# A new tail for the table of order and engine in an attention and feed-forward kernel

## The chip, the cores and the metric

The kernel runs on one core of one Trainium2 chip. The metric is the device time of one execution in microseconds (us), the median of several runs. Five instruction streams matter: TensorE (PE; its weight loads are listed as PEld), VectorE (DVE), ScalarE (ACT), GpSimd (POOL) and SyncE (SP), which issues the transfers.

## The reference

`q`, `k` and `v` have the shape (4, 8, 768, 64): batch, heads, sequence, head size. Six sign bits of a projection put every query and key into a bucket, only pairs in one bucket attend, and the result goes through a feed-forward layer with Mish.

```python
mask = q_bucket[:, :, :, None] == k_bucket[:, :, None, :]
scores = scale * np.matmul(q, k.transpose(0, 1, 3, 2))
scores = np.where(mask, scores, -1000000000.0)
scores = scores - np.max(scores, axis=-1, keepdims=True)
attn = np.exp(scores)
attn = attn / (np.sum(attn, axis=-1, keepdims=True) + 1e-09)
attn_out = np.matmul(attn, v)
x = attn_out.transpose(0, 2, 1, 3).reshape(B * S, H * D)   # 3072 x 512
h = x @ w_in                                               # 512 -> 2048
g = h * np.tanh(softplus(h))
out = g @ w_out                                            # 2048 -> 512
```

## The kernel before

Numbers are split into a high and a low fp16 part, and a product is three fp16 matmuls (high by high, high by low, low by high). The tokens are worked in 12 units of 256 tokens. A unit has eight steps of attention and eight of the feed-forward layer, and the feed-forward steps of a unit run while the attention of the next one does. Unit 0 is done in fp32 while the weights are split.

The names below are those of the operations in the code.

- **S0 to S95** (`att_front`): the score products, 8 matmuls of line 894 each, into the one PSUM tile `ps_s` (three banks; some early ones use `ps_s2`). Then VectorE takes the maximum (line 906, `max`) and makes scale and bias (`scl`, lines 912 to 918), ScalarE takes two exponentials (line 932, `exp`), and only then may the next S overwrite the tile. `scl` is written as two VectorE instructions, as four shorter ones, or for GpSimd.
- After the exponentials come the reciprocal (954), a high part `hi` (line 387 on ScalarE, 388 on VectorE, 385 on GpSimd) and a low part `lo` (403) for each of the two heads, and a transposing transfer PT<-hl (420) on SP's queue.
- **V0 to V47** (`att_pv`): the value products, one for two S, 36 matmuls of line 1015 in 128 by 64 form, where nearly all others are 128 by 128. `x_hi` (1039, ScalarE) and `x_lo` (1042, VectorE) then empty their half of `ps_t`.
- **H0 to H95**, **O**: the first and second feed-forward products (lines 1075 to 1077; 1132 to 1134; in fp32 for unit 0, lines 1071 and 1128). Between them lie `mish` on ScalarE (1099), which needs another function table than the exponential, a high part (`g_hi`, 387 or 388) and a low part (`g_lo`, 403).
- Small things for the next batch or unit: sums of squares (437), their spread over the partitions by two small matmuls (`st`, 469 and 470, into `ps_t`), the step that reads them (`half`, 473), the hash products (`hp`, 728) with their bits (736) and the transfers KT<-tok and QT<-tok (420).

The order is written out. `op` records each of the 2978 operations with the engines that may do it and what must come before it. `ORDER` lists their numbers in the order in which they are issued, with a letter where it isn't the first engine that does it; `ordered` walks through it:

```python
for w in ORDER.split():
    n, a = (int(w[:-1]), "abcd".index(w[-1])) if w[-1].isalpha() else (int(w), 0)
    o = self.ops[n]
    yield o.alts[a][2]
```

Every engine takes its own operations in that order and waits for what it needs, so an operation that waits holds up all that stands behind it on its engine. Some entries are optional: `pre_e` and `pre_m` load a function table ahead of time, or do nothing in their second form, and `fill` is a set of 8 idle matmuls or nothing.

Of the kernel before, what the change touches and what calls it, by code (L numbers as in the profile page):

```python
# [99 lines left out]
404b 322 331 332 368b 413 511b 334 424b 335b 343 336c 337 414 512b 354b 355 362 363 357 369b 345 338 339 370b 356b 364  # L100
358 514b 359 420 223b 476 479 513 946b 366 371 367 344 386 394 374c 210b 478 532 372 387 375 360 361 373 389b 388b 395
425 505 506 396 390 481 376b 491 380b 515 381 377 398 391 392 399 426b 427 434 435 378 382 533 534 535 379 446b 428b
429 436b 531 393 488 530 438 430 439 536b 493 539b 468c 490 431 537c 432 433 440c 383 441 482 447 469 384 638 483 484b
385 470 448b 472 486 442 487 450b 473 594 494 597 540 443 516 497c 492b 471b 538 549 596 444 445 548 541 599 550 280b
551 474 451 452c 498 455b 449 406 453 500b 456 475 552 517 518b 604 499 1132b 457b 501 458 553b 556 554b 365b 545b
680b 520 407 454 558 607 521 559 555 503 557 495 405 585 542 522d 560 502 460 610 523 543 459 586 525 524b 461 587 544
526 588 464b 462b 973b 546 528 589 463 590c 465 466c 467 591 547 397b 609 527 504 584 569 561c 562 592b 624 756b 593
612 757b 408 758b 759b 570 409 563b 564b 571 641 529 565 572 626 642 627 760b 761b 625 762b 763b 764b 765b 766b 767b
768b 769b 770b 771b 772 773b 774b 628 775b 643 573 629 411 410 630 567 633c 631c 566 574 227b 665 676 575 576c 666 577
644 645 412 568 634 632 578 579 582 668 667 776 601 646 496 669 580 583 670 600 602 603 671b 674 672b 704 705 673 647b  # L110
648b 605 606 616c 613 581 693 675 650 706 713 684 694 649 685 635 651 617 618c 620b 695 686 683 737 636 687 637b 688b
# [12 lines left out]
1031 1032 959 903c 994 915 1096 906 1018 1019 1020 907 908 1083b 1631 1034 1035 938 1042b 1033 1051 1040 1052 1551b
909 1487b 1053 1626b 1011b 1240 1062 1064 995 1145 1036 1037 1055 996 997 998c 1000 1056 1070 1001 910 1131 1334b 1071
1072c 1133 1242 1141 931b 1136 1080 1074 1081 1082 1104 1138 1139c 1065c 1066 1140 1054 1134b 1073 1076 1085 1067 1148
1084 1097 1086 1087 1088c 1105 1106 1090 1115 786b 1068 1075 1256b 1089 1098 1099 999 1002 1003 1102 1004 1005 1153
1135 1169 1356b 1092 1101 1107b 1116 1108 1150 1077 1109c 1130 1170 1186 1091 1110c 1151b 1155 1185 1111 1119 1117
1118 1120 1121 1069 1006 1142 1156b 1113 1152 1208 1122 1123 1093 1124 1187 1112 1339b 1158 1154 1194 1125c 1128 1126
1195 1518 1143 1144 1157 1237 1146 1147 1171 1012 1161 1114 1159 1162 1163c 1160 1165 1129 1127 1209 1210 1164 1172  # L130
1173 1220 1176 1175 1177c 1211 1238b 1221 1379 1243 1167 1178 1179c 1027b 1188 1196 1181 1197 1198 1351b 1189 1190
1834 1248 1245 1259 1199b 1201 1246b 1247 1222 1250 1251c 1252 1380 1281 1297 1166 1180c 1183 1192 1193 1212 1213 1168
1214c 1216 1261 1444 1223 1224 1225 1228 1227 1202 1182 1215c 1218 1738b 1229b 1230 1262b 1263 1280 1296 1184 1231c
1233 1217 926 1264 1063b 1249b 1203 1137b 1232c 1266 1267b 1253 871b 1239 1254 1333 1255 1200c 1234 1204 1219 1338
1268 1335 1336b 1337 1235 1350 1257 1412 1206 1258 1272b 1282 1273 1340 1341b 1274 1244b 1283 1284 1286 1269 1236 1306
1275c 1276 1278 1287 1288b 1289 1290c 1292 1355 1299 1298 1305 1300 1149b 2311 1301 1307 1317 1205 1342 1352 1277 1291
1294 1100 1343 1332 1304 1303 1309b 1318 1279 1353b 1310 1270 1354 1381 1308 1319 1320 1311 1313 1293 1312 1315 1371
1382 1271 1322 1403 1372 1404 1323 1324b 1174b 1207 1295 1325 1326c 1328 1344 1357 1426 1314 1611b 1405 942 1316 1265b
1327 1345 1346 1360 1329 1358c 1349 1348 1383 1330 1331 1448 1376b 1359 1384 1385 2176b 1373 1361 1363 1364 1365 1386b
1387 1047b 1362 1374 1375 1377 1367 1378 1438 1439 1471 1427 1428 1388 1389 1406 1447 1395 1396 1799b 1429 1474 1397c  # L140
1399 816b 1366 1369 1058 1472 1407 1390 1391 1479 1476 1477b 1478 1413 1392 1414 1514 1408 1415 1368 1398c 1393 1480b
1481 1482c 1400 1513 1370 1416 1615 1490 1394 1417c 1419 1401 1420 1483 1411 1410 1430b 1441 1431 1433c 1546 1722 1402
1492 1432 1493c 1494 1473 1442 1443 1545 1547 1434 1435 1418 1285b 1191 1449 1421 1422 1423 1424 1445 1436 1446 1450
1463b 1605 1464 1465 1437 1425 1607 1451 1452 1608b 1453 1454b 1467 1468 1466c 1484 1495 1497 710 1485 1609 1486 1456
1521 1488 1498c 1469 1470 1499 1500 1503c 1489 1505c 1504 1506 1501 1734b 892b 1502 1625 1627 1515 1516 1610 1508 1511
1507 1509 1517 1555 1612 1457 1522 1613c 1558c 1572 1559 1614 1520 1519 1630 1537c 1538 1539c 1512 1548 1556 1557 1554
1510 1576 1541 1542 1549 1458 1459 1604 1455 1523 1540 1550 1543 1544 1524 1525 1526 1527 1528c 1460 1628b 1461 1553
# [1141 lines left out]
```

## Time and profile before

| | us |
|---|---|
| median of 3 runs | 822.91 (821.88 to 824.8) |
| the profiled execution, its own time | 822.01 |
| its span, first to last instruction | 820.2 |
| around the span | 1.8 |
| TensorE busy | 791.7 |
| VectorE busy | 700.9 |
| ScalarE busy | 661.7 |
| GpSimd busy | 64.0 |

Busy is the union of an engine's instructions. Matmuls overlap each other, so TensorE's busy time counts the time in which at least one is in flight. The granted clock of TensorE was 0.999 of the full 2.4 GHz over the span.

### The profile page before, as it was taken

To read this page: it belongs to the slowest core of one execution; us is meant where nothing else is said; L and a number is where in the kernel's file an instruction comes from. 1 tells how busy PE (TensorE), PEld (TensorE's weight loads), DVE (VectorE), ACT (ScalarE), POOL (GpSimd) and SP (SyncE) were. 2 spreads that over 40 slices of the span, in tenths; PEclk is the share of its full clock that TensorE was granted. 3 is DMA by queue.
4 is the path that set the end of the run, shared out by engine and by line. 5 is a ranking of instruction groups with operands and counts; after the bars stand their busy time and mean duration, and the time that the engine had idled before them with its cause. 6 is when DMAs were issued, how large, how long until landed. Compare 5 with 4: busy or idle time off the path is not lost. (4 is left out here: it accounts for less than half of the span.)

```text
span 820.2 us, 16787 instructions
## 1 busy us (share of the span) xinstructions
PE 791.7 (97%) x6588; PEld 547.3 (67%) x6588; DVE 700.9 (85%) x1349; ACT 661.7 (81%) x1000; POOL 64.0 (8%) x67
## 2 busy tenths in 40 slices
PE   6789999999999999999999999999999999999998
PEld 5566674666667676677677676676576577576664
DVE  6899999989889887889999888999899889789522
ACT  6899999989888789899797798788698788686312
POOL 3454441200000000000000000000000000000000
PEclk9999999999999999999999999999999999999999
DMA  9987979699999797999989779879979777866500
GB/s 266 274 248 223 230 180 188 141 164 215 177 178 172 144 185 129 157 190 189 214 155 200 152 131 178 167 130 215 181 143 196 141 109 125 142 118 128 109 1 26
DMA packets 400303, 135.58 MB, mean 165 GB/s; under 512 B 370528, under 2 KB 391008, under 8 KB 400224
## 3 DMA queue, kind: packets, MB, share of 16 engines
q1 hardware_dynamic: 400224, 134.52, 82.1%
q8 instruction: 51, 0.84, 0.4%
q14 instruction: 28, 0.23, 0.1%
HBM read 35.65 MB, written 6.29 MB: 51 GB/s over the span
## 5 line engine op out<-in xcount | busy, mean ns | idle before, releaser
L932 ACT ACTIVATE pb<-ps_s,svb 128x768 f32<-128x768 f32 x192 | 188.5, 986 | 38.2 <-DVE svb L918 31.4
L1075 PE MATMUL ps_acc<-X,wi 128*128 128x256 f16 x704 | 191.9, 273 | 1.0 <-ACT ffb L1099 1.0
L1077 PE MATMUL ps_acc<-X,wi 128*128 128x256 f16 x704 | 191.9, 273 | 0.0
L1076 PE MATMUL ps_acc<-X,wi 128*128 128x256 f16 x704 | 191.8, 273 | 0.0
L906 DVE TENSOR_REDUCE svb<-ps_s 128x2 f32<-128x1536 f32 x96 | 168.3, 1753 | 16.2 <-PE ps_s L894 14.8
L403 DVE SCALAR_TENSOR_TENSOR hl<-pb,svb,hl 128x768 f16<-128x768 f32 x175 | 176.2, 1014 | 6.5 <-ACT hl L387 4.4
L894 PE MATMUL ps_s<-KT,QT 128*128 128x512 f16 (+1 forms) x768 | 140.9, 326 | 7.5 <-ACT pb L932 2.8
L1132 PE MATMUL ps_o<-wo,ffb 128*128 128x512 f16 x352 | 133.5, 379 | 0.0
L1134 PE MATMUL ps_o<-wo,ffb 128*128 128x512 f16 x352 | 133.4, 379 | 0.0
L1133 PE MATMUL ps_o<-wo,ffb 128*128 128x512 f16 x352 | 133.4, 379 | 0.0
L894 PEld LDWEIGHTS <-QT 128*128 128x128 f16 x768 | 72.2, 97 | 56.1 <-issue 10.3
L1015 PE MATMUL ps_t<-PT,VT 128*64 128x256 f16 x1584 | 94.8, 274 | 2.2 <-DVE X L1042 1.5
L1099 ACT ACTIVATE ffb<-ps_acc,smalls 128x512 f32<-128x512 f32 x88 | 59.2, 684 | 43.9 <-PE ps_acc L1077 29.9
L1015 PEld LDWEIGHTS <-VT 128*64 128x64 f16 x1584 | 83.9, 110 | 16.1 <-issue 15.7
L387 ACT ACTIVATE hl<-pb,svb 128x768 f16<-128x768 f32 x78 | 71.7, 929 | 25.2 <-DMA PT<-hl 14.0
L1076 PEld LDWEIGHTS <-wi 128*128 128x128 f16 x704 | 68.8, 98 | 13.8 <-issue 1.6
L1075 PEld LDWEIGHTS <-wi 128*128 128x128 f16 x704 | 68.8, 98 | 12.1 <-issue 1.4
L1077 PEld LDWEIGHTS <-wi 128*128 128x128 f16 x704 | 68.8, 98 | 8.0
L403 DVE SCALAR_TENSOR_TENSOR ffb<-ffb,smalls 128x512 f16<-128x512 f32 x88 | 64.9, 746 | 3.3 <-ACT ffb L387 2.2
L1134 PEld LDWEIGHTS <-ffb 128*128 128x128 f16 x352 | 34.4, 98 | 41.5
L1133 PEld LDWEIGHTS <-ffb 128*128 128x128 f16 x352 | 34.4, 98 | 37.2
L1132 PEld LDWEIGHTS <-ffb 128*128 128x128 f16 x352 | 34.4, 98 | 34.2 <-issue 1.8
(208 smaller groups left out, 1038.2 us busy)
## 6 DMA issues: line engine op xcount, KB each, us to landing
out_dram<-ffb SPq DMA_DIRECT2D x24, 256.0 KB, 2.8
stg<-in_q_dram SPq DMA_DIRECT2D x10, 512.0 KB, 5.0
stg<-in_k_dram SPq DMA_DIRECT2D x12, 384.0 KB, 3.9
stg<-in_v_dram SPq DMA_DIRECT2D x12, 384.0 KB, 4.3
wo<-in_moe_w_out_dram SPq DMA_DIRECT2D x7, 512.0 KB, 4.3
stg<-in_moe_w_out_dram SPq DMA_DIRECT2D x7, 512.0 KB, 4.5
stg<-in_moe_w_in_dram SPq DMA_DIRECT2D x6, 512.0 KB, 5.3
wi<-in_moe_w_in_dram SPq DMA_DIRECT2D x6, 512.0 KB, 5.2
```

What stands on the lines that cost most here:

```text
L387: ACT=lambda: nc.scalar.activation(dst, src, AF.Copy, scale=sc),
L403: return [("DVE", 215 + 1.035 * n, port(lambda: nc.vector.scalar_tensor_tensor(out=dst, in0=src, scalar=sc, in1=hi, op0=ALU.mult, op1=ALU. ...
L894: nc.tensor.matmul(sc[:, hh * S + c0 * P:hh * S + c1 * P], QTb[:, u % 2, sl, qi], KTb[:, j, sl, hh * NCH + c0:hh * NCH + c1].rearrange("p ...
L906: op("max", [("DVE", 1790, lambda: nc.vector.tensor_reduce(out=sv[:, 0], in_=sc.rearrange("p (h e) -> p h e", h=2), axis=AX.X, op=ALU.max, ...
L932: EXP[n, hh] = op("exp", [("ACT", 1075, lambda hh=hh, t=t: nc.scalar.activation(pb[:, t], sc[:, hh * S:(hh + 1) * S], AF.Exp, bias=sv[:, 2 ...
L1015: nc.tensor.matmul(pv[hh * D:(hh + 1) * D, 0:256], vt[:, w, hh * NCH + c], pt[:, hh, a * NCH + c].rearrange("p s t -> p (s t)"), start=(x ...
L1075: nc.tensor.matmul(o, wh, X[:, 0, c], start=(c == 0), stop=False)
L1076: nc.tensor.matmul(o, wh, X[:, 1, c], start=False, stop=False)
L1077: nc.tensor.matmul(o, wl, X[:, 0, c], start=False, stop=(c == NCC - 1))
L1132: nc.tensor.matmul(PS[f"o{s}"], gh, hi[:, e], start=first, stop=False)
L1133: nc.tensor.matmul(PS[f"o{s}"], gh, lo[:, e], start=False, stop=False)
L1134: nc.tensor.matmul(PS[f"o{s}"], gl, hi[:, e], start=False, stop=last)
```

## The change

Only the string `ORDER` changes. Its first 361 entries are the same, which take about 66 us; from there to the end the entries are the same operations in another order and in part on other engines. No operation is added or removed, and TensorE does the same 556 groups of work (96 S, 48 V, 96 H, 192 O, 12 fills and the small ones). One line of 111 that differ:

```diff
-404b 322 331 332 368b 413 511b 334 424b 335b 343 336c 337 414 512b 354b 355 362 363 357 369b 345 338 339 370b 356b 364
+404b 223b 343 345 334 335b 413 322 331 545b 492b 280b 332 1132b 354c 336c 511 414 337 368b 355 573b 512b 638b 227b 356
...
```

Counted over the whole table, before and after: high parts of the attention weights 78, 87 and 11 on ScalarE, VectorE and GpSimd, now 76, 93 and 7; `scl` as two VectorE instructions 74, as four 20, now 66 and 28; high parts of the values 12 on ScalarE and 4 on VectorE, now 8 and 8; copies of the queries' high part 8 on ScalarE and 3 on VectorE, now 3 and 8; high parts of the feed-forward step 51 on ScalarE and 37 on VectorE, now 49 and 39; function tables loaded 108, now 117. The value products stand directly behind one another in 4 places, and now in 6.

Two places on VectorE show what moves. The first is ahead of S16, the first score product of unit 2, near 130 us. `L732` sums the hash product of that unit's queries, `L736` writes its bits into the token tile, which the transfer QT<-tok then turns; `L906`, `L912`, `L918` are the maximum and the scale step of S15, `L473` and `L458` the step behind a `st`. Before:

```order
L732 TENSOR_REDUCE hsum<-ps_t 128x96
L906 TENSOR_REDUCE svb<-ps_s 128x2
L403 SCALAR_TENSOR_TENSOR hl<-pb,svb,hl 128x768
L912 TENSOR_SCALAR svb<-svb,smalls 128x2
L918 TENSOR_TENSOR svb<-svb 128x2
L473 TENSOR_SCALAR hwo<-ps_t 128x2
L736 TENSOR_SCALAR tok_65<-hsum 128x16x6 x2
L458 TENSOR_SCALAR smalls<-hwo 128x2
L403 SCALAR_TENSOR_TENSOR hl<-pb,svb,hl 128x768
```

Now:

```order
L403 SCALAR_TENSOR_TENSOR hl<-pb,svb,hl 128x768
L732 TENSOR_REDUCE hsum<-ps_t 128x96
L906 TENSOR_REDUCE svb<-ps_s 128x2
L473 TENSOR_SCALAR hwo<-ps_t 128x2
L912 TENSOR_SCALAR svb<-svb,smalls 128x2
L918 TENSOR_TENSOR svb<-svb 128x2
L458 TENSOR_SCALAR smalls<-hwo 128x2
L736 TENSOR_SCALAR tok_65<-hsum 128x16x6 x2
```

The low part (`L403 hl`) between the maximum and the scale step is gone from there; it stands now ahead of the hash sum, so that the bits follow the hash sum and the maximum more closely. On TensorE, five O of unit 0 stand between S15 and S16 where there were four and two fills.

The second place is around S72 and V34, near 583 us. `L1042 X` is the `x_lo` that frees the half of `ps_t` that V34 writes; `L906` in the first list is the maximum of S72, and in the second the first `L906` is that of S71 and the last that of S72. Before:

```order
L388 TENSOR_SCALAR hl<-pb,svb 128x768
L403 SCALAR_TENSOR_TENSOR hl<-pb,svb,hl 128x768
L906 TENSOR_REDUCE svb<-ps_s 128x2
L912 TENSOR_SCALAR svb<-svb,smalls 128x2
L918 TENSOR_TENSOR svb<-svb 128x2
L782 TENSOR_REDUCE smalls<-smalls 128x1
L403 SCALAR_TENSOR_TENSOR hl<-pb,svb,hl 128x768
L473 TENSOR_SCALAR smalls<-ps_t 128x2
L1042 SCALAR_TENSOR_TENSOR X<-ps_t,smalls,X 128x256
L458 TENSOR_SCALAR smalls<-smalls 128x2
```

Now:

```order
L906 TENSOR_REDUCE svb<-ps_s 128x2
L912 TENSOR_SCALAR svb<-svb,smalls 128x1 x2
L916 TENSOR_SCALAR svb<-svb 128x1 x2
L736 TENSOR_SCALAR tok_65<-hsum 128x12x6
L403 SCALAR_TENSOR_TENSOR hl<-pb,svb,hl 128x768
L403 SCALAR_TENSOR_TENSOR ffb<-ffb,smalls 128x512
L1042 SCALAR_TENSOR_TENSOR X<-ps_t,smalls,X 128x256
L388 TENSOR_SCALAR hl<-pb,svb 128x768
L948 TENSOR_SCALAR svb<-svb 128x2
L403 SCALAR_TENSOR_TENSOR hl<-pb,svb,hl 128x768
L403 SCALAR_TENSOR_TENSOR ffb<-ffb,smalls 128x512
L906 TENSOR_REDUCE svb<-ps_s 128x2
```

`x_lo` stood behind the maximum of S72, a low part (`L403 hl`) and the `L473` of a `st`; it stands now ahead of the maximum of S72, behind the low part of an earlier step and a `g_lo`.

## Rows read from the trace of the kernel before

**Rows 1.** The page: busy time by engine; the chain that ended last.
```profile
PE 791.7 (97%) x6588; PEld 547.3 (67%) x6588; DVE 700.9 (85%) x1349; ACT 661.7 (81%) x1000; POOL 64.0 (8%) x67
...
PE 29%; DVE 1%; DMA 1%; ACT 0%; issue 0%; ACTq 0%
```

**Rows 2.** Windows: length, then busy us of each engine, clock, DMA share.
```profile
core 0: us, PE busy (x) PEld busy (x) DVE busy (x) ACT busy (x) POOL busy (x), PEclk, DMA share, GB/s
66.00:217.00 151.00, 143.79 (x1020) 96.79 (x1016) 144.47 (x256) 140.42 (x216) 32.99 (x26) 1.00 0.89 188
217.00:342.00 125.00, 124.33 (x1068) 85.95 (x1064) 108.87 (x214) 106.86 (x158) 0.00 (x0) 1.00 0.84 159
342.00:771.00 429.00, 426.18 (x3641) 293.71 (x3637) 381.97 (x723) 348.33 (x527) 0.00 (x0) 1.00 0.86 160
771.00:820.20 49.20, 45.24 (x330) 30.58 (x330) 12.10 (x20) 11.35 (x15) 0.00 (x0) 0.99 0.06 22
```

**Rows 3.** Waits of TensorE from 66 to 217 us: total, times, longest.
```profile
PE ps_s L894 <- ACT pb L932: 2.4, 4, 1.2
PE ps_s L894 <- DMA QT<-tok: 1.5, 1, 1.5
PE ps_acc L1075 <- ACT ffb L1099: 1.0, 2, 0.7
PE ps_t L469 <- ACT wo L437: 0.9, 1, 0.9
PE ps_t L1015 <- DMA PT<-hl: 0.4, 1, 0.4
PE ps_t L1022 <- ACT PT L978: 0.3, 1, 0.3
PE ps_t L1015 <- DVE hwo L473: 0.3, 1, 0.3
```

**Rows 4.** Waits of TensorE from 217 to 342 us, same columns.
```profile
PE ps_s L894 <- DVE smalls L458: 0.7, 1, 0.7
```

**Rows 5.** Waits of TensorE from 342 to 771 us, same columns.
```profile
PE ps_t L1015 <- DVE X L1042: 1.5, 1, 1.5
PE ps_t L728 <- DMA KT<-tok: 0.6, 1, 0.6
PE ps_s L894 <- ACT pb L932: 0.4, 1, 0.4
PE ps_t L469 <- ACT tok L437: 0.3, 1, 0.3
```

**Rows 6.** Timeline of VectorE: start, us, line, operation [idle before <-releaser].
```profile
583.39 0.15 DVE L782 TENSOR_REDUCE smalls<-smalls 128x1 f32<-128x4 f32 x1
584.65 1.02 DVE L403 SCALAR_TENSOR_TENSOR hl<-pb,svb,hl 128x768 f16<-128x768 f32 x1 [1.12 <-ACT hl L387]
585.59 0.15 DVE L473 TENSOR_SCALAR smalls<-ps_t 128x2 int32<-128x2 int32 x1
585.66 0.47 DVE L1042 SCALAR_TENSOR_TENSOR X<-ps_t,smalls,X 128x256 f16<-128x256 f32 x1
```

**Rows 7.** Timeline of TensorE: one value product alone, two in a row.
```profile
332.57 0.38 PE L1133 MATMUL ps_o<-wo,ffb 128*128 128x512 f16 x1
332.78 0.38 PE L1134 MATMUL ps_o<-wo,ffb 128*128 128x512 f16 x1
333.09 2.15 PE L1015 MATMUL ps_t<-PT,VT 128*64 128x256 f16 x36
335.18 0.18 PE L469 MATMUL ps_t<-smalls,ones 128*128 128x2 bf16 x1
...
437.84 0.38 PE L1134 MATMUL ps_o<-wo,ffb 128*128 128x512 f16 x1
438.15 4.12 PE L1015 MATMUL ps_t<-PT,VT 128*64 128x256 f16 x72
442.20 0.39 PE L894 MATMUL ps_s<-KT,QT 128*128 128x512 f16 x1
```

**Rows 8.** Timeline of TensorE around score product 16.
```profile
136.93 0.61 PE L1081 MATMUL ps_acc<-ones 128*128 128x128 bf16 x8
137.37 0.49 PE L894 MATMUL ps_s<-KT,QT 128*128 128x512 f16 x2
139.32 1.15 PE L894 MATMUL ps_s<-KT,QT 128*128 128x512 f16 x6 [1.45 <-DMA QT<-tok]
140.71 1.95 PE L1128 MATMUL ps_o<-wo,ffb 128*128 128x512 f32 x4
142.60 0.63 PE L1015 MATMUL ps_t<-PT,VT 128*64 128x256 f16 x8
```

**Rows 9.** Groups from 66 to 217 us: count, busy us, mean ns, idle before.
```profile
L388 DVE TENSOR_SCALAR hl<-pb,svb 128x768 f16<-128x768 f32 x5 | 3.1, 616 | 0.1
L912 DVE TENSOR_SCALAR svb<-svb,smalls 128x2 f32<-128x2 f32 x13 | 2.9, 224 | 0.3
L918 DVE TENSOR_TENSOR svb<-svb 128x2 f32<-128x2 f32 x13 | 2.1, 160 | 0.5
L912 DVE TENSOR_SCALAR svb<-svb,smalls 128x1 f32<-128x1 f32 x10 | 1.7, 209 | 0.1
L916 DVE TENSOR_SCALAR svb<-svb 128x1 f32<-128x1 f32 x10 | 1.7, 208 | 0.0
L388 DVE TENSOR_SCALAR ffb<-ffb,smalls 128x512 f16<-128x512 f32 x4 | 1.9, 474 | 0.0
L388 DVE TENSOR_SCALAR wi<-wi,smalls 128x1024 f16<-128x1024 f32 x3 | 2.2, 746 | 0.0
...
L385 POOL TENSOR_SCALAR hl<-pb,svb 128x768 f16<-128x768 f32 x11 | 15.7, 1431 | 33.3 <-DVE svb L954 18.3 <-DMA PT<-hl 8.2 <-ACT wi L437 6.7
```

**Rows 10.** Timeline of ScalarE around one table load.
```profile
408.38 0.19 ACT L932 ACTIVATION_READ_ACCUMULATOR pb<-ps_s,svb 128x1 f32 x1
408.59 1.28 ACT L1098 ACT_TABLE_LOAD   x1
409.88 0.69 ACT L1099 ACTIVATE ffb<-ps_acc,smalls 128x512 f32<-128x512 f32 x1
```

More of the change, by code (lines that the diff above doesn't have):

```diff
@@ new lines @@
+1153 1135 1169 1356b 1092 1101 1107b 1116 1108 1150 1077 1109c 1130 1170 1186 1091 1110c 1151b 1155 1185 1111 1119
+1117 1118 1120 1121 1069 1006 1142 1156b 1113 1152 1208 1122 1123 1093 1124 1187 1112 1339b 1158 1154 1194 1125c 1128
+1126 1195 1518 1143 1144 1157 1237 1146 1147 1171 1012 1161 1114 1159 1162 1163c 1160 1165 1129 1127 1209 1210 1164
+1172 1173 1220 1176 1175 1177c 1211 1238b 1221 1379 1243 1167 1178 1179c 1027b 1188 1196 1181 1197 1198 1351b 1189
+1190 1834 1248 1245 1259 1199b 1201 1246b 1247 1222 1250 1251c 1252 1380 1281 1297 1166 1180c 1183 1192 1193 1212 1213
@@ new lines @@
+1500 1394 1421 1605 1433c 1482c 1483 1435 1446 1484 1497 1503b 1513 1436 1437 1673 1463 1418c 1653b 1607 1496b 1422
+1464 1465c 1466c 1469 1470 1449 1450 1615 1467 1514 1493b 1423 1424 1468 1285 1451 1485 1452 1453 1454b 1486 1425
+1498c 1504 1456 1608c 1609 1546 1489 1488 1494 1625 1347b 1505c 1506 1507 1508 1515 1516 1517b 1555 1556 1519 1509
+1499 1940b 1520 1511 1557 1455c 1457 1522 1521 1610 1627 1510 1548 1545 1512 1547 1612 1458 1616 1537b 1538 1539c 1549
+1541 1523 1524 1501 1550b 710 1502 1558c 1459 1630 1540c 1543 1613c 1553 1552 1554 1525 1569 1568 1648 1560 1780b
@@ new lines @@
+1743b 1491b 1561 1632 1722b 1628b 1562 2231b 1542 1461 1526 1527 1460 1528c 1544 1462 1530 1570 1614 1531 1572 1563
+1564 1565 1629 1571 1566 1559 1575 1604 1635 1573 1576 1636 1633c 1574 1637 1596 1597 1598 1634 1599 1664 1600 1649
+1567 1619 1602 1601 1620 1621 1532 1665 1666 1701 1529 1577 1638c 1533 1578 1579 1687 1603 1591 1580 1623 1624 1650
+1581 1535 1582b 1688 1689 1534 1640b 1584 1651 1641 1642 1643 1690 1652 1654 1718 1644 1655 1585 1536 1726 1645 2059
+1586 1583 1480b 1674 1622b 1587 1646 1667 1721 1668 1656 1728 1719 1657 1658c 1669 1675 1676 1729c 1723 1660 1618
@@ new lines @@
+1860c 1863 1884 1939 1960 1941 1942c 2013 1931b 1932 1864 2061 1944 1943 1872 1873 1892 1893 1895c 1903 2014b 1886
+1894c 1896 2062 2063 1902 2015 1817b 1904 2089b 1898 1919 1899 1897 1905b 1885 1961 1887 2064 1946 1947b 2167 2018
+2016c 1949 1907 1908 1933 2017 1909b 1910 1911c 2023 1913 1934 1935 1912c 1948 1915 2030 1977 1976 1950 1937 1938
+1952b 1953 1954c 1956 2020 1962 1963 1978 1763 1997 2035 1964 1914 1955 1967 1966 1968c 1958 1969 1951 1916 1970c 1972
+1979 2032 1957 2037 1971 1965 1980 1981 1984 1983 1989c 2065 2021c 1985 2012 2038c 2033c 2022 2039 2066b 1986 1990
@@ new lines @@
+2310 2248 2284 2254 2299 2243c 2276 2246 2294 2300 2205 2206 2277 2207 2278c 2307 2280 2301 2328 2344 2329 2247 2281
+2345 2312 2308b 2309 2315 2019 2279 1982 2282 2283 2208c 2210 2209c 2304 2303 2155b 2316 2330 2346 2320 2321 2322
+2318c 2296 2211 1829b 2124b 2317 2255 2368 2331 2332 2239 2509b 2334 2324 2369 2367 2370 2335 2313c 2336b 2297 2337
+2338 2387b 2323 2256 2340 2326 2406 2347 2212 2353 2325 2314 2348 2213 2408 2257 2258 2409b 2401 2259 2422 2604b 2403
+2404b 2417 2327 2341 2339c 2349 2352 2351 2384 2342 2214 2260 2405 2261 2262c 2371c 2343 2264 2398 2265 2271 2373b
@@ new lines @@
+2460 2683 2682 2720 2721 2774b 2704 2731 2747 2749 2756 2684 2685 2686c 2687 2688 2690 2768 2703 2705 2706 2709 2708
+2733 2689 2723b 2724 2667 2423b 2691 2722 2668 2725 2727 2757 2734 2735 2551b 2950 2645 2758 2759 2955b 2738 2737
+2739c 2785 2786 2769b 2740 2726c 2728 2742c 2745 2746 2729 2730 2894 2788 2750 2793 2751 2752b 2741c 2790 2791b 2743
+2744 2932 2753b 2804 2889 2945b 2795 2796c 2797 2792 2754 2809 2755 2806 2771 2760 2761 2762c 2764 2811 2878 2826 2825
+2707 2772 2773b 2775 2763c 2807c 2766 2765 2776 2805 2777b 2798 2778 2779c 2781 2799 2800 2808 2880 2443 2767 2782
@@ L211 @@
+2879b 2919b 2920 2933 2925 2937 2770 2911b 2936 2938 2939 2514 2926 2949 2928 2171b 2934b 2929b 2930 2951 2944 2935
+2941 2943 2946 2952b 2953 2947c 2948 2959 2940 2942 2716b 2954 2915 2917 2031b 2912 2964 2966 2956 2694b 2961 2962c
+2963 2965 2967 2957c 2958 2968 2970 2971 2972b 2973 2969 2974 2976 2975b 2977
 """
```

187 lines of the change are left out of this document (77 added, 110 removed).

## The prediction, made before the changed kernel ran

> **What bounds the kernel now.** I read the page's busy times first [rows 1]. TensorE is busy 791.7 of 820.2 us, and the chain that ended last names it almost alone. So the question is not what any engine costs on average but where TensorE stands still, and whether the new order adds or removes such places. The windows [rows 2] cut the changed part into three and leave the tail. From 66 to 217 us TensorE is idle for 151 - 143.79 = 7.2 us, and VectorE has only 6.5 us to spare and ScalarE 10.6: three engines are nearly full, because the weights are split there. From 217 to 342 us TensorE is idle for 0.7 us, and from 342 to 771 us for 2.8 of 429. There VectorE has 47 us to spare and ScalarE 81. In the last 49 us TensorE runs at its own pace into the closing stores.
>
> All that a new order can win by waits is therefore 7.2 + 0.7 + 2.8 = 10.7 us, and two thirds of it lie in the stretch where VectorE is full. What it can lose has no such limit. The granted clock is 1.00 of 2.4 GHz in three windows and 0.99 in the tail [rows 2], so it plays no part.
>
> The lists of waits name nearly all of that idle time: eleven waits and 6.8 us in the first stretch [rows 3], one in the second [rows 4], four in the third [rows 5].
>
> **The change part by part.** TensorE's work is the same but for how often it changes form.
>
> *Changes to value products.* A value product alone costs two changes [rows 7]: the last O matmul starts 0.21 us after the one ahead of it, but V starts 0.31 after it, 0.10 more; and V then takes 335.18 - 333.09 = 2.09 us until the next product starts. Two V in a row take 442.20 - 438.15 = 4.05, where two alone would take 4.18. A pair thus saves 0.10 + 0.13, about 0.2 us. Two more pairs give **-0.4 us**. The bounds are narrow: 0.3 and 0.5.
>
> *342 to 771 us, waits that go.* All four listed waits [rows 5] sat at places where the order is now different. V34 waited 1.5 us for `x_lo` of V32. VectorE's rows show why it was late [rows 6]: `x_lo` (start 585.66) stood behind a low part that had waited 1.12 us for ScalarE's high part. The second pair of order lists has `x_lo` ahead of the maximum of S72, and so ahead of that low part and its wait: this one goes. The hash product that waited 0.6 us for KT<-tok stood directly behind H32; now H33, a `st` and H34 stand between, and one H is 24 matmuls at 0.11 us each, 2.6 us. S50 waited 0.4 us for its exponential with 4.6 us of other products since S49; now an O is added there. The `st` that waited 0.3 us for a sum of squares is moved too. I take all four as gone: **-2.8 us**. What is late next: in each of the four places, what follows on TensorE is ready. But some 400 us of new order make new waits, and these rows can't show where. The bounds are 0, and as many as the old order had times two, 5.6 us. I take a bit over half of the old, **+1.7 us**, since by my count the shortest distances are no worse: S to next S is 4.6 us of other work in 11 places before and in 11 now, and V stands at least 13.7 us of TensorE work behind its second S from V15 on, where the least was 13.0.
>
> *217 to 342 us.* From S31 to S42 the order is nearly the same, the 0.7 us wait [rows 4] included: **0**. VectorE has 16 us to spare there [rows 2]. It needs about 3.5 us more by S31, by the count of its instructions, and I cover that with this spare time; if it weren't there, the 3.5 us would be seen in full.
>
> *66 to 217 us, one wait that shrinks.* S16 stood still for 1.5 us in its middle for QT<-tok [rows 3, 8]. Now one more O of unit 0 and no fills stand ahead of it: an O takes up to 1.9 us with the change to V that follows it (140.71 to 142.60), two fills at most 0.4 us each (136.93 to 137.37), so S16 has about 1 us more to cover, or somewhat more. On VectorE the bits that the transfer needs stand closer behind the hash sum (first pair of lists), but the hash sum itself is later; by adding up VectorE's instructions from the start of the change, the bits come some 0.6 us later. I take the difference as **-0.7 us**, between 0 and -1.5.
>
> *66 to 217 us, more work on VectorE.* Until S26, which starts at 217.1 us, I counted what VectorE must have done in either order. It has six more high parts, about 0.62 us each (one of weights 0.75) [rows 9]: +3.8. Four scale steps are written as four short instructions (2 x 0.209 + 2 x 0.208 = 0.83) in place of two (0.224 + 0.160 = 0.38): +1.8. Three fewer high parts of the feed-forward step, 0.474 each: -1.4. The small ones give -0.2. That is +4.0 us in nine more instructions; instructions on VectorE begin about 0.08 us before the one ahead ends (584.65 + 1.02 against 585.59) [rows 6], which leaves **+3.2 us**. ScalarE's sum is the same within 0.2 us, and GpSimd does four high parts less, which took it 1.4 us each and for which it waited 33 us in all [rows 9]. So work goes from the one engine with time to spare to the fullest one. The cover is VectorE's 6.5 us of idle time. If it takes all of the new work, the cost is nothing, or a gain where a slow GpSimd step no longer holds up a transfer; if nothing fits, it is the whole 3.2. Four of the score products in this stretch waited for the exponentials that follow VectorE's scale step [rows 3], so the slack is thin. I take **+1.2 us**, a bit over a third, with ends at -2 and +3.2.
>
> *Function tables.* Nine more loads on ScalarE, 1.28 us each by the row [rows 10], 11.5 us. By the order, the additional ones fall behind 500 us, where ScalarE has most of its 81 us to spare [rows 2], or in the tail, where it is busy 11 of 49 us: **0**. If each stood in the chain from an S to the next, it would cost the full 1.28.
>
> The sum: -0.4 - 2.8 + 1.7 + 0 - 0.7 + 1.2 + 0 = **-1.0 us**. It applies to the profiled execution's 822.0 us (820.2 of span and 1.8 around it) and gives 821.0; against the median of the runs, 822.9, it gives 821.9. I put it in between, at **821.5 us**.
>
> About 0.3%, 2.5 us, is what a measurement of this kernel can tell from no change: faster means under 820.4, slower over 825.4.
>
> **The rivals.**
>
> *Faster: the order fits throughout.* The four later waits go and few new ones come (+0.5 in place of 1.7), and of the 7.2 us that TensorE idles from 66 to 217 us some 3 go, because high parts that waited on GpSimd are done at once elsewhere. That gives -0.4 - 2.3 - 3 = -5.7, about 817 us. For it speaks that VectorE's 6.5 us of idle time would hold all of the new work twice over; against it that VectorE is 96% busy there and gets more.
>
> *Slower: VectorE decides the first stretch.* If its idle time stays 6.5 us, because it is made of short waits at fixed places, S26 comes 3.2 us late and S31 3.5 us, and nothing gives it back, since TensorE is full from 217 us on. With -0.4 and new waits as long as the old ones (0): 822.9 + 3.1 is 826 us. It decides from the point at which less than about 1 of those 3.2 us finds room. Against it: ScalarE's part and the order of the low parts are eased at the same time.
>
> *Slower: the tables stand in the chain.* Near the end a load stands between an exponential and the high part behind it, though one did so before. If all nine were on TensorE's path, 822.9 + 11.5 = 834 us. Against it: only TensorE's 2.8 us of waits from 342 to 771 us name ScalarE at all, 0.7 us of them. The Trainium skill's ScalarE page (ScalarE: Activation LUTs, What ACT_TABLE_LOAD costs) gives a further drain of about 1.38 us to each load, 2.66 in all, by which nine would take 24 us of ScalarE. The trace doesn't agree: the load starts at 408.59, takes 1.28, and the next activation starts at 409.88 [rows 10].
>
> *No change that can be seen* is my forecast's own case: many small sums of both signs.
>
> **How the numbers follow.** The forecast, within 2.5 us of before: 0.43. Faster: 0.37, since four waits are seen to go and only guesses come in their place. VectorE as the bound: 0.16, and the tables: 0.04, together 0.20 for slower. The range reaches from the faster rival's 817, less 0.5 for a ramp that gains a little more, to the slower one's 826: 816.5 to 826.
>
> **What would show it.** TensorE's waits from 342 to 771 us should not name `X` L1042 with 1.5 us nor KT<-tok behind H32, and should sum to about 2. From 66 to 217 us (to the start of S26) TensorE's idle time should stay at 7 to 8 us; QT<-tok should wait under 1 us; VectorE should be busy for 147 to 148 us. V pairs should stand in six places at 4.05 us. If S26 starts after 220 us, the second rival is right; before 215, the first. A table load just ahead of an exponential for which an S waits would show the third. I would be wrong altogether if new waits of a kind that these rows don't show, such as transfers that land later because others are issued ahead of them, came to more than 3 us.

## The result, and the profile after

The changed kernel takes 829.8 us (median of 4 runs, 827.62 to 830.74), before on the same chip 822.62: a ratio of 1.0079 (95% interval 1.005 to 1.0108). It is slower by some 6.5 us, and outside the predicted range. The profiled execution takes 829.13 us with a span of 827.2, 7.0 more than before.

The page of the changed kernel: busy time by engine, and the chain that ended last.

```profile
PE 793.9 (96%) x6588; PEld 548.6 (66%) x6588; DVE 704.1 (85%) x1383; ACT 664.3 (80%) x1002; POOL 60.1 (7%) x62
...
PE 52%; DVE 12%; ACT 7%; DMA 5%; issue 2%; SPq 0%; ACTq 0%; DVEq 0%
```

Against [rows 1] no engine has much more to do. What has changed is the chain: it leaves TensorE more often. The shares of the two pages can't be compared as they stand, since the chain of before reaches back only to 562 us (its shares make 31%) and that of the changed kernel to 174 us (78%). From 568 us on, where both have one, TensorE holds 241 of 249 us before and 212 of 256 now, VectorE 6 and now 26, transfers none and now 11.

The windows of the changed kernel, cut at the same points of the program as [rows 2]:

```profile
66.00:219.70 153.70, 144.13 (x1030) 96.86 (x1028) 149.40 (x265) 141.33 (x218) 29.33 (x23) 1.00 0.89 188
219.70:343.60 123.90, 123.90 (x1056) 85.42 (x1052) 109.17 (x212) 103.80 (x157) 0.00 (x0) 1.00 0.81 158
343.60:777.80 434.20, 428.03 (x3642) 295.11 (x3638) 382.76 (x753) 348.42 (x523) 0.00 (x0) 1.00 0.86 157
777.80:827.20 49.40, 45.21 (x331) 30.54 (x330) 9.22 (x15) 15.90 (x21) 0.00 (x0) 1.00 0.06 22
```

The lengths differ from [rows 2] by +2.7, -1.1, +5.2 and +0.2 us, 7.0 together. In the first stretch TensorE now idles 153.7 - 144.13 = 9.6 us, where it was 7.2, and VectorE is left 4.3 us, where it was 6.5. In the third TensorE idles 6.2 us, where it was 2.8.

TensorE's waits in that third window, total, times and longest:

```profile
PE ps_t L728 <- DMA QT<-tok: 2.4, 1, 2.4
PE ps_s L894 <- ACT pb L932: 1.6, 4, 0.7
PE ps_t L1015 <- DMA PT<-hl: 1.2, 1, 1.2
PE ps_acc L1075 <- ACT ffb L1099: 0.8, 2, 0.5
```

None of the four waits of [rows 5] stands in its old place: that part of the prediction came true. But new ones take more than their room. The largest is a hash product that waits for QT<-tok. Here it is on TensorE's timeline (start, us, operation, idle before it), where the reader should look at what comes behind it too:

```profile
363.14 0.58 PE L728 MATMUL ps_t<-pj,QT 128*128 128x12 f16 x16 [2.40 <-DMA QT<-tok]
363.58 0.38 PE L1075 MATMUL ps_acc<-X,wi 128*128 128x256 f16 x1
363.75 0.42 PE L1076 MATMUL ps_acc<-X,wi 128*128 128x256 f16 x1
363.96 0.42 PE L1077 MATMUL ps_acc<-X,wi 128*128 128x256 f16 x1
...
366.69 0.27 PE L1075 MATMUL ps_acc<-X,wi 128*128 128x256 f16 x1
366.80 0.27 PE L1076 MATMUL ps_acc<-X,wi 128*128 128x256 f16 x1
```

H36's matmuls start 0.21 us apart instead of 0.11 until 366.5: TensorE stood still for 2.40 us, and then ran at half clock. The window from 363.0 to 366.6 says so, at 0.53 of 2.4 GHz:

```profile
363.00:366.60 3.60, 3.46 (x31) 2.59 (x32) 2.15 (x6) 1.39 (x2) 0.00 (x0) 0.53 1.10 235
```

H36's 24 matmuls take 1.47 us longer than at full clock. So this one place costs 2.40 + 1.47 = 3.9 us. It isn't the whole loss: the one run of the four whose mean granted clock was 1.000 took 827.62 us, still 5 us over before, and the others, at 0.996 to 0.998, took 829.1 to 830.7.

Why the transfer is late is seen on SP's queue. First before, then after (start, us on the queue):

```profile
350.84 1.45 SPq L420 DMA_TRANSPOSE KT<-tok  x1
353.59 1.79 SPq L420 DMA_TRANSPOSE QT<-tok  x1
355.47 2.02 SPq L420 DMA_TRANSPOSE PT<-hl  x1
```

```profile
351.42 5.29 SPq L420 DMA_TRANSPOSE PT<-hl  x2
356.82 1.72 SPq L420 DMA_TRANSPOSE QT<-tok  x1
358.64 2.30 SPq L420 DMA_TRANSPOSE KT<-tok  x1
```

KT<-tok is issued 7.8 us later than before, and QT<-tok 3.2 us later, both behind two PT<-hl that hold the queue for 5.29 us. Of either delay 1.6 us is the whole program's: S42 starts that much later. VectorE is caught as well. Its copy of the queries' high part, which the new table takes from ScalarE here, waits for KT<-tok with everything behind it:

```profile
364.38 0.43 DVE L397 COPY tok<-tok 128x1024 f16<-128x1024 f16 x1 [2.58 <-DMA KT<-tok]
```

And the transfers themselves take longer. From issue to landing, in the same 24 us of the program, before and after (count, median us):

```profile
PT<-hl SPq DMA_TRANSPOSE x6, 3.9
KT<-tok SPq DMA_TRANSPOSE x2, 4.4
QT<-tok SPq DMA_TRANSPOSE x2, 4.5
```

```profile
PT<-hl SPq DMA_TRANSPOSE x6, 4.7
KT<-tok SPq DMA_TRANSPOSE x2, 5.4
QT<-tok SPq DMA_TRANSPOSE x1, 6.3
```

The first stretch, waits of TensorE from 66 to 219.7 us; beside [rows 3] the wait for QT<-tok went from 1.5 to 0.4, and that of the score products for their exponentials from 2.4 to 4.6:

```profile
PE ps_s L894 <- ACT pb L932: 4.6, 5, 1.4
PE ps_t L469 <- ACT wi L437: 1.3, 2, 0.7
PE ps_t L1015 <- DMA PT<-hl: 1.1, 2, 0.9
PE ps_t L728 <- DVE X L1042: 0.9, 1, 0.9
PE ps_s L894 <- DMA QT<-tok: 0.4, 1, 0.4
```

### The profile page after: what moved, and what is told of

It is laid out like the page before. It is cut to its first block, busy times and chain, and to the rows that moved or that the text cites. A ratio compares the mean times of both kernels' runs of the same rounds, so it can differ in the third digit from the quotient of the medians.

```text
span 827.2 us, 16807 instructions
## 1 busy us (share of the span) xinstructions
PE 793.9 (96%) x6588; PEld 548.6 (66%) x6588; DVE 704.1 (85%) x1383; ACT 664.3 (80%) x1002; POOL 60.1 (7%) x62
## 4 chain that ended last, share of the span: by engine, by line
PE 52%; DVE 12%; ACT 7%; DMA 5%; issue 2%; SPq 0%; ACTq 0%; DVEq 0%
PE ps_s L894 8%; PE ps_t L1015 7%; PE ps_o L1132 7%; PE ps_o L1134 6%; PE ps_o L1133 6%; PE ps_acc L1075 6%; PE ps_acc L1076 6%; PE ps_acc L1077 6%; DVE svb L906 3%; DVE hl L403 3%; DMA PT<-hl 3%; ACT pb L932 3%; DVE hl L388 1%; ACT hl L387 1%; DVE ffb L403 1%
## 5 line engine op out<-in xcount | busy, mean ns | idle before, releaser
L403 DVE SCALAR_TENSOR_TENSOR hl<-pb,svb,hl 128x768 f16<-128x768 f32 x175 | 178.3, 1025 | 6.1 <-ACT hl L387 4.5
L906 DVE TENSOR_REDUCE svb<-ps_s 128x2 f32<-128x1536 f32 x96 | 168.1, 1751 | 9.5 <-PE ps_s L894 9.0
L403 DVE SCALAR_TENSOR_TENSOR ffb<-ffb,smalls 128x512 f16<-128x512 f32 x88 | 64.8, 745 | 21.4 <-ACT ffb L387 20.5
L387 ACT ACTIVATE hl<-pb,svb 128x768 f16<-128x768 f32 x76 | 69.6, 930 | 14.6 <-DMA PT<-hl 6.9
L1134 PEld LDWEIGHTS <-ffb 128*128 128x128 f16 x352 | 34.4, 98 | 42.2 <-DVE ffb L403 0.9
L388 DVE TENSOR_SCALAR hl<-pb,svb 128x768 f16<-128x768 f32 x93 | 57.7, 625 | 2.8 <-DMA PT<-hl 1.4
L1133 PEld LDWEIGHTS <-ffb 128*128 128x128 f16 x352 | 34.4, 98 | 36.7
```

Source lines behind the costliest of these rows:

```text
L387: ACT=lambda: nc.scalar.activation(dst, src, AF.Copy, scale=sc),
L403: return [("DVE", 215 + 1.035 * n, port(lambda: nc.vector.scalar_tensor_tensor(out=dst, in0=src, scalar=sc, in1=hi, op0=ALU.mult, op1=ALU. ...
L906: op("max", [("DVE", 1790, lambda: nc.vector.tensor_reduce(out=sv[:, 0], in_=sc.rearrange("p (h e) -> p h e", h=2), axis=AX.X, op=ALU.max, ...
L1133: nc.tensor.matmul(PS[f"o{s}"], gh, lo[:, e], start=False, stop=False)
L1134: nc.tensor.matmul(PS[f"o{s}"], gl, hi[:, e], start=False, stop=last)
```

## The experiments

Two theories stood at first. **Transfers:** the loss lies in single places, above all the middle piece, where transfers are issued late. **VectorE:** the loss is the work given to VectorE in the full first stretch. A third was open: that of the function tables. Ratios are to before on the same chip; 0.001 is 0.8 us.

| kernel | median us | ratio, 95% interval |
|---|---|---|
| e1_first | 824.39 | 1.0008, 0.9995 to 1.0022 |
| e2_middle | 827.11 | 1.0047, 1.003 to 1.0063 |
| e3_last | 823.75 | 1.0008, 0.9994 to 1.0022 |
| e4_queue | 829.4 | 1.0071, 1.0055 to 1.0087 |
| e5_hp_later | 827.54 | 1.0052, 1.0036 to 1.0068 |
| e6_engines | 839.93 | 1.0204, 1.0179 to 1.0229 |
| e7_orderonly | 848.76 | 1.0307, 1.0284 to 1.0329 |
| e8_mends | 822.25 | 0.9991, 0.9978 to 1.0004 |
| e9_copy_later | 828.56 | 1.0068, 1.005 to 1.0087 |
| e10_v35 | 828.32 | 1.0064, 1.0046 to 1.0082 |
| e11_before_mended | 823.45 | 1.001, 0.9996 to 1.0025 |
| e12_turns_early | 830.41 | 1.0094, 1.0075 to 1.0112 |
| e13_old_middle | 825.06 | 1.003, 1.0016 to 1.0044 |
| e14_turn_late | 830.43 | 1.0083, 1.0062 to 1.0104 |

**Which piece.** The table differs in three pieces, between which the same operations have been issued in both orders, so each can be taken alone.

```diff
-before
+before[:361] + after[361:1107] + before[1107:]     (e1_first)
+before[:1386] + after[1386:1793] + before[1793:]   (e2_middle)
+before[:1927] + after[1927:]                       (e3_last)
+after[:1386] + before[1386:1793] + after[1793:]    (e13_old_middle)
```

> The new order only up to S30 (entries 362 to 1107 of the table), the old one from there. In the two traces S31 to S40 start 2.4 us later than before. If VectorE's added work in the first stretch makes that, this is 2 to 3 us over before, and TensorE idles 9 to 10 us up to S26 in place of 7.2. If the loss is all from transfers that land late later on, or from the function tables, it is within 1 us of before.

> The new order only between S41 and S54 (entries 1387 to 1793). In the traces this stretch loses 3.9 us net: 2.4 us of a wait for QT<-tok, 1.5 us of matmuls at half the clock right behind that wait, some waits of 0.4 to 0.7 us, against 1.9 us of old waits that go. If a stretch's loss is its own, this is 3.5 to 4.5 us over before, with the same wait and the same dip of the clock. If the wait came from the state in which the first stretch left the queues, it is not here, and the time is 1 us or more under before.

> The new order only from S59 on (entries 1928 to the end); seven of the nine added table loads lie here. In the traces this stretch loses 0.5 us: V34's wait of 1.5 us goes, V35 waits 1.5 us for PT<-hl, and smaller ones come. If that is its own, this is within 1 us of before. If the tables cost, each up to 1.28 us, it is 2 us or more over before.

> The changed kernel with the order of before in the middle piece alone (S41 to S54, 342 to 446 us). Theory A (the middle piece holds the loss, 3.5 us by itself and 2 to 2.5 more where the new first piece stands ahead of it): 823.5 to 824.5 beside before's 823, as the first and last pieces alone, each about 0.5 us over. Theory B (what the first piece loses on VectorE shows in full when the middle piece is well): 825.5 to 827.

The middle piece alone costs 0.0047, 3.9 us; the first and the last 0.7 us each, neither distinct from nothing. With the old middle piece the changed kernel is at 1.003: of its 6.5 us over before some 4 are gone, and 2.5 are left. Against before, theory A gave 0.5 to 1.5 us over and theory B 2.5 to 4: the 2.5 stand at the lower edge of theory B, so more of the loss lies outside the middle piece than I had taken. The traces show where. S8 stands ahead of the change and S42 at the start of the middle piece; their rows on TensorE, first before, then after:

```profile
63.66 1.46 PE L894 MATMUL ps_s<-KT,QT 128*128 128x512 f16 x8
342.12 1.47 PE L894 MATMUL ps_s<-KT,QT 128*128 128x512 f16 x8
```

```profile
63.59 1.46 PE L894 MATMUL ps_s<-KT,QT 128*128 128x512 f16 x8
343.76 1.46 PE L894 MATMUL ps_s<-KT,QT 128*128 128x512 f16 x8
```

From S8 to S42 is 278.46 us before and 280.17 after. The same in three stretches and for the exchanged pieces, us more than in the trace of before:

| trace | S8 to S42 | S42 to S58 | S58 to the end |
|---|---|---|---|
| changed kernel | +1.7 | +4.6 | +0.7 |
| e1_first | +1.4 | -0.1 | +0.8 |
| e2_middle | -0.2 | +3.0 | +1.0 |
| e3_last | 0.0 | 0.0 | +1.4 |
| e13_old_middle | +1.6 | -0.2 | +1.0 |

The first piece therefore has a price of its own: in the eight traces with it (these and those of the kernels below) S8 to S42 takes 1.0 to 2.3 us more than in the trace of before, in the four others with the old one from 0.8 less to 0.1 more. With before itself that is 1.8 us apart in the mean. In the last column e1_first and e2_middle, with the old order there, are as long as the changed kernel, so it shows no clear loss of the last piece. Alone and in company the middle piece isn't quite the same: by itself its hash product waits 1.6 us for QT<-tok and the half clock doesn't come; behind the new first piece it waits 2.40 and 1.47 follow.

```profile
PE ps_t L728 <- DMA QT<-tok: 1.6, 1, 1.6
```

The last piece also holds the additional table loads: from 500 us on e3_last loads 54 tables, before 44 and the changed kernel 55 (the four groups of ACT_TABLE_LOAD added up). Its time is within 0.0022 of before.

**Places in the middle piece.** In the first edit QT<-tok (1420) goes ahead of a PT<-hl (1402) on SP; in the second the waiting hash product (1421) goes behind H36 (1605); in the third, on top of it, the copy (1418) and the hash sum (1422) go later on VectorE; in the fourth, on top of that, V35 (2368) and its `x_hi` (2369) go behind an O (2367).

```diff
-1402 1420 1500            (e4_queue)
+1420 1402 1500
...
-1421 1605 1433c           (e5_hp_later)
+1605 1421 1433c
...
-1418c 1653b 1607 1496b 1422 1464 1465c 1466c 1469 1470 1449      (e9_copy_later)
+1653b 1607 1496b 1464 1465c 1466c 1422 1469 1470 1418c 1449
...
-2368 2331                 (e10_v35)
...
-2369 2367 2370
+2367 2368 2369 2370
```

> The changed kernel with one entry moved: the transfer QT<-tok for unit 6 is issued ahead of a PT<-hl that stood before it on SP's queue. In the trace its data were ready at 354.7 us and it was issued at 356.8, behind a pair of PT<-hl that held SP for 5.3 us. If the queue makes the 2.4 us wait, the wait shrinks to under 0.5 us, the clock stays up behind it, and the time falls by 2.5 to 4 us against the changed kernel. If the transfer itself lands late because the DMA engines are full, the wait stays over 1.5 us, and the time within 1 us.

> The changed kernel with one entry moved: the hash product that waits 2.40 us for QT<-tok at 363.1 us is issued behind H36 instead of ahead of it. Theory A (its place on TensorE costs 2.47 us of standing still and, by the half clock behind that, 1.47 us more in H36): 3.9 us less than the changed kernel, 825.5 to 826, and H36's matmuls at 0.109 us a step. Theory B (the transfer queue is the limit, as when the two transfers were exchanged): the same wait turns up behind H36 or at the next value product, and the time stays above 828.5.

> The kernel with the hash product behind H36, and on VectorE the copy of the next queries' high part, which waits 2.26 us there for KT<-tok with everything behind it, moved behind the reciprocal, two high parts, the hash sum and a low part. Theory A (the copy is given to VectorE by the new table and holds up S44's maximum, so that S45 stands still for 1.76 us): that wait is gone, S46 starts 1.5 to 2 us earlier against its own start, and the time is some 1.7 us less, 825.8 beside 827.5. Theory B (S45 is late for another reason, say its exponential on ScalarE): S45 still waits over 1 us and the time stays within 0.6 us.

> The same, and V35, which waits 1.25 us for PT<-hl near 593 us (1.54 us with what else stops in it), moved behind the next feed-forward product. Theory A (its place ahead of the landing is all): the wait is gone and the time is some 1.4 us less than with the copy moved alone, about 824.4. Theory B (what follows V35 on the other engines, the low part of S74 and the hash product, is late next): S74 or the value products up to V37 wait by as much, and the time stays within 0.5 us.

With QT<-tok ahead, the hash product no longer waits, but V20 does, for the PT<-hl that was put behind, and half clock follows there too; the time is as long as before the exchange:

```profile
PE ps_t L1015 <- DMA PT<-hl: 2.5, 1, 2.5
```

With the hash product behind H36 the wait and the half clock are gone, and S44 starts about 4 us earlier against the score products ahead of it. Then S45 stands still, because VectorE still waits for KT<-tok and its maximum comes late, and with it the exponential (the row names a `g_hi` of VectorE that ended at the same moment). Of that kernel a row of the waits from 343 to 450 us, and one of VectorE's timeline:

```profile
PE ps_s L894 <- DVE ffb L388: 1.6, 1, 1.6
```

```profile
365.26 0.43 DVE L397 COPY tok<-tok 128x1024 f16<-128x1024 f16 x1 [2.26 <-DMA KT<-tok]
```

So 3.9 us were to be had and about 2 were won by the ratio, 1.0052 beside 1.0079; the intervals overlap, but the trace shows both halves. With the copy moved out of the way too, S45 waits 0.7 us, and a small product 1.9 us for a square on ScalarE, which in the code must come behind the copy, and so is late with it: VectorE now waits 2.90 us for PT<-hl ahead of the copy. No time was won (1.0068):

```profile
PE ps_t L469 <- ACT tok L437: 1.9, 1, 1.9
```

V35's move took its wait for PT<-hl away and nothing off the time (1.0064): a `st` near 604 us and H43 lose 0.6 us each in that trace, where they lost none in the one of the copy moved alone. Of four expectations of theory A one was half right and three were wrong.

**Both transfers early, and one late.** The reverse test is the sharper one. The first kernel is the changed one with KT<-tok (1394) and QT<-tok (1420) early again, and V20 (1500) and the hash product (1421) later. The second is before, with nothing but the chain of KT<-tok late: its hash product (1390) behind H34 (1490), hash sum and bits (1391 to 1393) behind the low part, the transfer behind two others.

```diff
-1479 1370 1440 1410       (e12_turns_early)
+1479 1390 1391 1392 1393 1370 1440 1394 1410
...
-1419 1490 1390 1391 1400 1393
+1419 1420 1490 1400
...
-1402 1420 1500 1394 1421 1605
+1402 1605 1421
...
-1484
+1484 1500
```

```diff
-1407 1390 1391 1479       (e14_turn_late, on before)
+1407 1479
...
-1490 1394
+1490 1390
...
-1401 1420
+1401 1391 1392 1393 1420
...
-1402
+1402 1394
```

> The changed kernel, with the two transfers of the next batch as early in SyncE's queue as before had them: the hash product of the keys behind H33 instead of H34 with its bits and KT<-tok right behind it, QT<-tok straight behind its low part and ahead of two PT<-hl, and for that the second hash product behind H36 and V20 behind S44. Theory A (KT<-tok and QT<-tok stand too late in the queue, and the copy on VectorE, the square on ScalarE, the hash product and S45 all wait for them): of the waits at 350 to 375 us no more than 1 us is left, VectorE's 2.6 us of idle time for KT<-tok is gone, and the time is 3.5 to 4.5 us under the changed kernel, 825 to 826 beside before's 823. Theory B (the queue is full in this piece whatever comes first): as much waiting turns up at V20 or V21, and the time stays above 827.5.

> Before, with one thing of the new middle piece: the hash product of the keys behind H34 (2 products later than its place behind H32), its hash sum and bits behind the low part of the queries, and KT<-tok behind QT<-tok and two PT<-hl. Theory A (the late KT<-tok is what costs): the 0.6 us wait behind H32 goes, but the copy of the queries' high part, here on ScalarE, waits 2 us or more for KT<-tok with the exponential of S43 behind it, S44 to S46 come late, and the time is 2 to 3.5 us more than before, 825 to 826.5. Theory B (it is not this transfer): within 1 us of before.

One late transfer within the old order costs 0.0083, 6.8 us: as much as the whole change. Its rows: one of ScalarE's timeline, one of TensorE's waits from 343 to 450 us, and two windows.

```profile
363.74 1.04 ACT L396 COPY tok<-tok 128x1024 f16<-128x1024 f16 x1 [5.20 <-DMA KT<-tok]
```

```profile
PE ps_t L469 <- ACT tok L437: 5.8, 1, 5.8
```

```profile
364.00:369.90 5.90, 0.12 (x3) 0.04 (x2) 1.54 (x6) 5.87 (x11) 0.00 (x0) 0.73 0.98 182
369.90:373.50 3.60, 3.60 (x16) 1.94 (x16) 2.72 (x5) 3.54 (x5) 0.00 (x0) 0.50 0.43 82
```

In the old order the copy is ScalarE's; it waits 5.20 us for KT<-tok, the square behind it is late, a `st` on TensorE waits 5.8 us for the square, and TensorE comes back at half clock. The 0.6 us of [rows 5] is gone, as the prediction had it for this very move, and ten times as much has come. I had expected 2 to 3.5. It shows what a late KT<-tok can cost; in the changed kernel the path is another, since the copy is VectorE's there and the longest wait is for QT<-tok.

The other kernel won nothing. KT<-tok is issued at 353.32 and VectorE's wait for it is gone, but a run of four PT<-hl then fills the queue, and VectorE waits longer, for those. SP's and VectorE's rows:

```profile
359.21 9.98 SPq L420 DMA_TRANSPOSE PT<-hl  x4
```

```profile
364.97 0.62 DVE L388 TENSOR_SCALAR hl<-pb,svb 128x768 f16<-128x768 f32 x1 [4.17 <-DMA PT<-hl]
```

It speaks for theory B: in the new middle piece some transfer is late whichever goes first.

**VectorE's share of the first stretch.** Engines and order of the first piece were exchanged for one another: before's order with the new engines for 64 operations, and the new order with the old engines. Two of the 64 (a high part and a scale step):

```diff
-356b
-364
+356
+364b
```

> The order of before, with the engines of the new table for the 64 pieces of work of the first changed stretch (66 us to S30) that it gives to another engine or writes in another form. Theory A (the engines make the stretch longer: VectorE's added 3.2 us find little room): VectorE is busy some 147 us in the stretch, S26 starts 2 to 3 us later than in before, and the time is 1 to 2.5 us more. Theory B (it is the order that costs): S26 within 0.8 us of before, time within 1 us.

> The new order of the first changed stretch (66 us to S30) with the engines of before, and before from there on: the other half of the first stretch. Theory A (the engines cost): S26 within 0.8 us of before, and S16 stands still for about 0.5 us for QT<-tok. Theory B (the order costs): S26 2 to 3 us late, and the waits for the exponentials at S11, S14 and S18, 1.2 to 1.5 us each, are there with these engines too.

Both are far slower, by 17 and 25 us, and neither theory foresaw that. TensorE idles 151 - 137.62 = 13.4 and 151 - 130.97 = 20.0 us from 66 to 217 us, the largest part for exponentials; the first lines of their waits from 66 to 232 us, of each kernel:

```profile
PE ps_s L894 <- ACT pb L932: 6.5, 6, 2.2
```

```profile
PE ps_s L894 <- ACT pb L932: 8.7, 7, 2.1
```

So in this full stretch the order and the engines can't be priced apart. Together, as the first piece, they cost 0.7 us by e1_first's ratio and about 1.8 by the traces. VectorE's load as the cause of that is neither shown nor excluded.

**Mending the old kernel.** First x_lo (2182) ahead of S72's maximum (2300) and the hash product of the keys (1390) behind H33 (1479), with its hash sum (1391) later too; then, on top, the `half` step (2260) ahead of the high part and O70 (704) ahead of S16 (601).

```diff
-1390 1391 1479            (e8_mends)
+1479 1390
...
+2182 2300
...
+704 601                   (e11_before_mended)
...
+2260 2279
```

> Before, with two small moves on the grounds of the prediction: x_lo of V32 ahead of the maximum of S72 on VectorE, and the hash product that waits for KT<-tok behind H33 instead of ahead of it. Theory A (a wait that goes is time that goes): V34's 1.5 us and the hash product's 0.6 us are gone, and the time is 2 us less than before, about 821 to 821.5 beside 823 to 823.5. Theory B (what goes there comes back in the waits that follow): within 0.7 us of before, with the starts of S72 to S95 first earlier and then not.

> Before with the two moves of the mended kernel (x_lo ahead of the maximum of S72, the hash product behind H33) and two more: the step that reads the small sums ahead of the high and low part, since V34 still waited 0.73 us for it, and an O of unit 0 ahead of S16 instead of behind it. Theory A (all of these waits are only a matter of place): S16's 1.45 us and V34's last 0.7 us are gone, S26 starts 1 to 1.5 us earlier, and the time is 3 us under before, some 820 to 820.5 beside 823. Theory B (in the full first stretch nothing is to be had by place, because S16's maximum then comes 0.4 us later on the full VectorE): S26 within 0.5 us of before, and the time as with two moves, 1 to 1.5 us under before.

The first kernel has 0.7 us of the expected 2 (0.9991, not distinct from before), and of the 0.9 us by which its trace is shorter 0.8 lie between S8 and S42, where its order is that of before: V34 waits 0.7 us for the next late thing, and a `st` 0.4 us for the hash sum that now stands close ahead of it. In the second S16's wait is gone, but the first stretch isn't shorter: V7 waits 2.0 us for PT<-hl and runs at half clock for a moment. First the one kernel's waits from 342 to 771 us, then the other's from 66 to 220:

```profile
PE ps_t L1015 <- DVE smalls L473: 0.7, 1, 0.7
...
PE ps_t L469 <- DVE hsum L732: 0.4, 1, 0.4
```

```profile
PE ps_t L1015 <- DMA PT<-hl: 2.2, 2, 2.0
```

No kernel here beats before beyond its interval.

## Why the prediction was wrong

**New waits, +1.7 us: the step that failed.** All four old waits went, and the third window still idles 6.2 us; with the 1.47 us of half clock the new waits come to 7.7 us, over the bound of 5.6. The exchanged pieces put most of it in the middle piece: 3.9 us when it stands alone, some 4 when it is taken out. The statement that the granted clock plays no part failed with it. The ground for the small figure was that the shortest distances were no worse, from S to S and from V to its second S. Those are distances to VectorE and ScalarE. I did not measure the distance from a transfer's issue to its reader, nor a transfer's turn in SP's queue, though the prediction named just this as what would make it wrong altogether; but among its rivals such waits had no chance of their own. And the move that I credited with 0.6 us, the hash product behind H34, is the head of the chain that issues KT<-tok: e14_turn_late shows that this chain alone, late, costs 6.8 us in the old order. That the move freed TensorE was seen; that its followers on VectorE, SP and ScalarE moved with it wasn't followed.

**Waits that go, -2.8: right** [rows 5], though not a gain one keeps. Where two of them were taken out by themselves (e8_mends), the ratio gave 0.7 us of their 2.1, within its noise.

**S16's wait, -0.7: right in kind,** -1.1 measured (1.5 to 0.4 in the list [rows 3]).

**VectorE's added work, +1.2: too small in the trace.** VectorE is busy 149.40 us, where I had said 147 to 148 [rows 2], and its idle time took up 2.2 of the 4.9 us that were added. S26 starts some 2.7 us later, in spite of the 1.1 won at S16. TensorE's idle time grew by 2.4 us there, so its other waits grew by 3.5, over this term's end of 3.2; how much of that is VectorE's isn't shown. The second window gives 1.1 back, 0.7 of it the wait of [rows 4], which I had put down as unchanged. This is the slower rival's pattern, but not its price of 3.1 us: about 1.8 by the traces, and 0.7 by the first piece's ratio, with an interval from -0.4 to +1.8.

**Value products, -0.4: right.** A pair takes 4.06 us in the changed kernel (441.81 to 445.87), as in [rows 7].

**Tables, 0: right** as far as shown. 117 are loaded, and e3_last, with ten more than before from 500 us on, can't be told from before. The load's price also held: in the changed kernel one starts at 353.84, takes 1.28 us, and the next activation starts at 355.13. The Trainium skill's page (ScalarE: Activation LUTs, What ACT_TABLE_LOAD costs) gives 2.66 us; these rows don't show the remainder.

What stays open: whether the new middle piece can be mended at all. Four kernels moved a wait from QT<-tok to PT<-hl, KT<-tok or a square without winning more than some 2 us. That one late transfer can cost this much is shown by e14_turn_late in the old order; that late transfers are the cause in the new order is argued from the waits, and one test of it (e12_turns_early) went against me. The 1.2 us by which the changed kernel exceeds the sum of its pieces' ratios (0.7 + 3.9 + 0.7) lie within their intervals; the traces would put them to the longer wait and the half clock behind the new first piece, and to the first piece itself, but that was read, not tried. Why the new first piece is slower also stays open.

## What to carry to other kernels

When an instruction is moved off the busiest engine's path, follow its descendants through the other queues to the next place where that engine reads them, transfers above all: here a hash product moved for 0.6 us went with a transfer issued 7.8 us later. A wait that is taken away in a nearly full stretch tends to turn up at the next late thing: here such moves gave 2.2 of 3.9 us (e5_hp_later), 0.7 of 2.1 (e8_mends, within the noise), or nothing (e4_queue, e9_copy_later, e10_v35). A wait of some 2 us on TensorE is to be priced with the half clock that may follow.

## What had not been expected of the hardware

The half clock behind a wait. In the 16 traces of this study, the first 10 us left out, TensorE stood still for 1.8 us or more 15 times. Eight times it came back at half clock or fell to it within about 1 us, with waits of 1.87, 1.94, 1.99, 2.21, 2.40, 2.49, 2.50 and 5.78 us; seven times it didn't, after 1.82 to 2.06 and one of 2.44. Of the 114 waits between 0.9 and 1.8 us two were followed by it within about 1 us, of 1.21 us (e12_turns_early) and 1.25 (e8_mends), and in e4_queue it came near 24 us behind stops of 0.5 to 0.7 us. Two of these windows, of e6_engines behind the 1.94 us and of e8_mends behind the 1.25:

```profile
605.70:609.10 3.40, 3.40 (x28) 2.38 (x25) 1.98 (x5) 0.47 (x1) 0.00 (x0) 0.50 0.55 103
30.30:33.60 3.30, 3.30 (x29) 3.18 (x28) 1.90 (x2) 0.94 (x3) 2.05 (x4) 0.50 0.87 169
```

So the length of a wait alone doesn't decide it. Nor does the order: from 24 to 32 us all 16 kernels have the same entries, and the half clock came there in four of the traces. It cost 1.47 us of H36 in the changed kernel and some 1.8 us of S44 and H35 in e14_turn_late.
